# A gated linear attention and feed-forward kernel: weights loaded among the first tile and half of the second, the state update delayed by one to three steps, e and ln written two tiles ahead

## The chip, the cores and the metric

One core of one Trainium2 chip. The metric is the device time of one execution in microseconds (us). The profile's span is shorter than that time, by about 1.8 us in both kernels; the profiled run of each is compared with the other's. All times told here are of the fast state: one execution each of st_one_instruction and weights_behind_two_tiles was slow (over 1.5% above the same kernel's fastest) and is left out. Engines: PE is TensorE, DVE VectorE, ACT ScalarE, POOL GpSimd; SP issues the DMAs.

## The reference, cut to what matters

```python
f = 1.0 / (1.0 + np.exp(-f_logit))                 # B, H, S, D = 4, 8, 768, 48
for t in range(S):
    state = f[:, :, t, :, None] * state + np.einsum('bhd,bhe->bhde', k[:, :, t], v[:, :, t])
    y[:, :, t] = np.einsum('bhd,bhde->bhe', q[:, :, t], state)
x = y as (B*S, H*D)                                # 3072 x 384
out = np.maximum(x @ w1, x @ w2) @ w_out           # w1, w2: 384 x 1024; w_out: 1024 x 384
```

The kernel cuts the sequence into 6 chunks of 128 for each of 4 batches: 24 tiles, tile i being chunk i // 4 of batch i % 4. So tile i needs the state that tile i - 4 left.

## The kernel before: the parts concerned

The order of instructions is written by hand as words, `op n`. A prologue runs once; then STEP runs for i = 1, 2, ... with `op n` meaning that op on tile i + n. Whatever has been done is skipped. Each engine works through its own instructions in this order (ACT's x, e and ln of one step of before start at 69.97, 70.34 and 70.90), and SP issues the loads in this order.

```python
STEP = """
lk 5  lf 7  e 1  lq 5  ln 1  cum 1  d0 -1  ed 1  fl 1  ei 1  g0 -1  a 0  am 0  v 1  d1 -1
g1 -1  kpv 1  lv 5  o0 -1  y 0  x 0  qp 1  sa 0  o1 -1  xT 0  tmp 0  st 0  tr 1  xTe 0  tre 1
ob -1  out -1
"""
```

What the words do, by engine (cut to one line each; `...` marks cuts):

```python
# SP    lf lk lq lv: one tile's loads, 192 KB each in rows of 192 B;  lw1 lw2 lwo: weights;  out: store
# ACT   e:  nc.scalar.activation(e, f, AF.Exp, scale=-1.0)
#       ln: nc.scalar.activation(ell[:, :, 0:D], e, AF.Ln, bias=1.0)
#       ei, ed, fl: AF.Exp of cum;   g0, g1: Relu of d;   x: copy of y;   w2ca, woc: casts of weights
# PE    cum: matmul(lhsT=ut, rhs=ell) + four 1-column matmuls;   tr: 8 transposes of kp, qp
#       a: q k^T by head;   y: old state and am against q, v;   sa: k^T v (nothing for chunk 5)
#       xT: 3 transposes of x;   d0, d1: 12 matmuls wd x xT each;   o0, o1: 6 + 5 matmuls
#       w2T, w2o: from the weights, once;   warm: matmuls on zeros, nobody reads them
# DVE   v: cast of v;   kpv: k * ei;   am: a * mask;   tmp: sa + old state
#       xTe, tre, ob: copies out of PSUM;   w2Te, wd: once, from the weights
# POOL  qp: q * ed;   wdp 0: w1 - w2 for the first third

def m_st(i):                                     # POOL, two instructions
    ...
        for o in range(2):
            r, e = slice(o * DP, (o + 1) * DP), slice(o * D, (o + 1) * D)
            nc.gpsimd.tensor_mul(st_b[b][(c + 1) % 2][r, :, e], st[i]["tmp"][r, :, e],
                                 st[i]["fl"][r, :].unsqueeze(2).to_broadcast([DP, NP, D]))
```

max(h1, h2) is computed as relu(x (w1 - w2)) + x w2; `wd` is w1 - w2, and `w2o` is w2 w_out, made once. The PSUM pools: three rotating buffers for the attention (cum, tr, y, xT, sa), one for a, three for d, o and the weights.

## Time and profile before

| | before |
|---|---|
| time, median of 3 runs (lowest to highest) | 150.71 us (150.70 to 150.85) |
| span of the profiled run | 148.87 us |
| first feed-forward matmul (`d`) | 26.11 us |
| first `d` matmul of tile 2 | 36.29 us |
| tile 2 to tile 21 | 96.53 us in 19 steps, nearly all 5.09 |
| tile 21 to the end | 16.05 us |

Read it as three stretches. The prologue ends where the `d` matmuls of the tiles begin to come at equal distances. In the equal steps, a small saving counts 19 times. The end is one tile deep and has nothing behind it to fill its gaps.

### The profile page before, as it was taken

What the parts mean: (1) busy time and instruction counts of PE and PEld (TensorE: products, weight loads), DVE (VectorE), ACT (ScalarE), POOL (GpSimd) and SP (SyncE); (2) the same over time, 40 slices, a digit from 0 to 9 for tenths busy, and PEclk for the clock granted to TensorE, in tenths of its full rate; (3) what the DMA queues carried; (4) which work ended last, traced back from release to release, by engine and by line L of the source; (5) the groups of instructions that cost most, each with busy time, mean ns of one, the idle gap of its engine ahead of it and who ended that gap; (6) DMA issues with size and microseconds to landing.
All of it is one profiled execution on the core that took longest, in us unless ns stands there. A gap on an engine that the chain in (4) does not pass through costs nothing.

```text
span 148.9 us, 4490 instructions
## 1 busy us (share of the span) xinstructions
PE 134.7 (90%) x1835; PEld 101.6 (68%) x1835; DVE 107.4 (72%) x189; ACT 89.5 (60%) x201; POOL 50.7 (34%) x81
## 2 busy tenths in 40 slices
PE   0369879899999999999999999999999999999981
PEld 0134456677788778877887887788778877777760
DVE  7837985288787779778877887787778777756621
ACT  3435182967757676757766676757676756764430
POOL 8222263214334334432533352345225432201000
PEclk9999999999999999999999999999999999999999
DMA  5999999999998989999799999999999996101111
GB/s 100 197 224 390 395 341 220 200 195 174 221 198 168 228 174 218 200 223 224 155 230 194 236 216 208 222 198 230 206 209 183 228 230 177 54 3 53 57 53 53
DMA packets 105236, 28.60 MB, mean 192 GB/s; under 512 B 100352, under 2 KB 104448, under 8 KB 105216
## 3 DMA queue, kind: packets, MB, share of 16 engines
q1 hardware_dynamic: 105216, 28.32, 90.0%
q8 instruction: 14, 0.23, 0.7%
q14 instruction: 6, 0.05, 0.1%
HBM read 23.59 MB, written 4.72 MB: 190 GB/s over the span
## 4 chain that ended last, share of the span: by engine, by line
PE 72%; ACT 2%; DVE 1%; issue 0%
PE o L325 26%; PE d L307 22%; PE tr L222 6%; PE a L240 5%; PE cum L189 4%; PE y L285 3%; PE y L280 2%; PE xtp L295 2%; PE sa L254 2%; PE cum L191 1%; ACT ell L180 1%; ACT x L290 1%; ACT e L176 1%; DVE ob L330 0%; DVE qp L215 0%; DVE xT L299 0%
## 5 line engine op out<-in xcount | busy, mean ns | idle before, releaser
L307 PE MATMUL d<-xT,wd 128*128 128x128 bf16 x576 | 40.0, 219 | 0.7 <-DVE xT L299 0.4
L325 PE MATMUL o<-wo,gT 128*128 128x384 bf16 x192 | 38.9, 326 | 0.4 <-ACT gT L314 0.4
L269 POOL TENSOR_TENSOR st<-tmp,fl 64x192 bf16<-64x192 f32 x40 | 20.4, 509 | 45.0 <-DVE tmp L262 43.5
L314 ACT ACTIVATE gT<-d 128x512 bf16<-128x512 f32 x48 | 29.0, 607 | 10.2 <-PE d L307 10.1
L307 PEld LDWEIGHTS <-wd 128*128 128x128 bf16 x576 | 32.6, 97 | 3.4 <-issue 0.6
L245 DVE TENSOR_TENSOR am<-a,mask 128x1024 bf16<-128x1024 f32 x24 | 29.4, 1224 | 6.4 <-PE a L240 6.3
L215 POOL TENSOR_TENSOR qp<-qt,ed 128x384 bf16<-128x384 f32 x20 | 20.0, 998 | 21.1 <-POOL st L269 10.9
L325 PEld LDWEIGHTS <-gT 128*128 128x128 bf16 x192 | 17.3, 98 | 10.1 <-ACT gT L314 0.8
L290 ACT CAST x<-y 128x384 bf16<-128x384 f32 x24 | 11.5, 479 | 19.2 <-PE y L285 19.2
L231 DVE COPY trs<-tr 128x1024 bf16<-128x1024 bf16 (+1 forms) x25 | 16.6, 669 | 4.5 <-PE tr L222 2.7
L201 ACT ACTIVATE ed<-cum 128x384 f32<-128x384 f32 x24 | 11.7, 489 | 11.2 <-POOL st L269 9.1
L299 DVE COPY xT<-xtp 128x384 bf16<-128x384 bf16 x24 | 8.5, 356 | 11.5 <-PE xtp L295 11.5
L262 DVE TENSOR_TENSOR tmp<-sa,st 128x384 f32<-128x384 f32 x20 | 11.1, 556 | 6.4 <-issue 6.4
L325 PE MATMUL o<-w2o,xT 128*128 128x384 bf16 x72 | 15.6, 326 | 0.0
L197 ACT ACTIVATE ei<-cum 128x384 f32<-128x384 f32 x24 | 11.9, 497 | 6.2 <-PE cum L191 6.1
L330 DVE COPY ob<-o 128x384 f32<-128x384 f32 x24 | 13.2, 548 | 3.2 <-PE o L325 3.2
L176 ACT ACTIVATE e<-ft 128x384 f32<-128x384 f32 x24 | 12.7, 529 | 3.1 <-DMA ft<-in_f_logit_dram 3.1
L189 PE MATMUL cum<-ell,ut 128*128 128x384 bf16 x24 | 8.1, 338 | 6.5 <-ACT ell L180 6.3
L180 ACT ACTIVATE ell<-e 128x384 bf16<-128x384 f32 x24 | 12.6, 524 | 0.8
L191 PEld LDWEIGHTS <-ell 128*128 128x128 bf16 x96 | 6.0, 97 | 8.3 <-issue 5.6
L285 PE MATMUL y<-vb,am 128*128 128x48 bf16 x192 | 11.2, 183 | 0.2 <-DVE am L245 0.2
L285 PEld LDWEIGHTS <-am 128*128 128x128 bf16 x192 | 9.6, 96 | 2.3 <-DVE am L245 0.7
(50 smaller groups left out, 178.9 us busy)
## 6 DMA issues: line engine op xcount, KB each, us to landing
vt<-in_v_dram SPq DMA_DIRECT2D x24, 192.0 KB, 4.4
ft<-in_f_logit_dram SPq DMA_DIRECT2D x24, 192.0 KB, 4.3
qt<-in_q_dram SPq DMA_DIRECT2D x24, 192.0 KB, 4.7
kt<-in_k_dram SPq DMA_DIRECT2D x24, 192.0 KB, 4.4
out_dram<-ob SPq DMA_DIRECT2D x24, 192.0 KB, 3.3
w_f<-in_moe_w_dram SPq DMA_DIRECT2D x6, 512.0 KB, 8.3
wo_f<-in_moe_w_out_dram SPq DMA_DIRECT2D x2, 768.0 KB, 8.2
```

What stands on the lines that cost most here:

```text
L176: nc.scalar.activation(e, ld[i]["f"].rearrange("p h d -> p (h d)"), AF.Exp, scale=-1.0)
L180: nc.scalar.activation(ell[:, :, 0:D], st[i]["e"].rearrange("p (h d) -> p h d", h=H), AF.Ln, bias=1.0)
L189: nc.tensor.matmul(out=ps[:, 0:dm], lhsT=ut, rhs=ell[:, :, 0:D], start=True, stop=True)
L215: eng.tensor_mul(s["qp"][:, :, 0:D], ld[i]["q"], s["ed"].rearrange("p (h d) -> p h d", h=H))
L231: nc.vector.tensor_copy(s["tr"][:, n:n + len(sel)], psum.pop(("tr" + sel, i)))
L245: nc.vector.tensor_mul(am.rearrange("p o n c -> p (o n) c"), psum.pop(("a", i)).rearrange("p o n c -> p (o n) c"), mask)
L269: nc.gpsimd.tensor_mul(st_b[b][(c + 1) % 2][r, :, e], st[i]["tmp"][r, :, e], st[i]["fl"][r, :].unsqueeze(2).to_broadcast([DP, NP, D]))
L285: nc.tensor.matmul(out=y[:, ds], lhsT=am[:, o, p, :], rhs=vb[:, ds], start=(c == 0), stop=(c == 0 or o == 1))
L307: nc.tensor.matmul(out=ps[:, n, :], lhsT=wd[:, j, f * C:(f + 1) * C], rhs=st[i]["xT"][:, j, :], start=(j == 0), stop=(j == JG - 1))
L314: nc.scalar.activation(s["g"][:, half * 4:half * 4 + 4, :], psum.pop(("d", half, i)), AF.Relu)
L325: nc.tensor.matmul(out=psum["o", i], lhsT=l() if callable(l) else l, rhs=r, start=(n == 0), stop=(n == len(mms) - 1))
L330: nc.vector.tensor_copy(t, psum.pop(("o", i)))
```

## The change

The intent: load the weights earlier, so that the feed-forward part can begin after one tile rather than two; and give the chain e, ln, cum and the chain sa, tmp, st more time. Nothing is computed otherwise; 6 warm-up matmuls are left of 19.

```diff
 PROLOGUE = """
-lv 0  lf 0  lf 1  lq 0  lk 0  lk 1  lq 1  lv 1  lw2 0  lw2 1  lwo 0  lw2 2  lwo 1  lw1 0
-lq 2  lw1 1  lw1 2  lf 2  lv 3  lk 2  lv 2  lf 3  lk 3  lf 5  lq 3  lf 4  lk 4  lq 4  setup 0
... (11 more lines of the old prologue)
+setup 0  setup 2  setup 1  lf 1  lf 0  lq 0  lw2 2  lk 0  lw2 0  lw2 1  lv 0  lwo 1  e 0
+lwo 0  e 1  ln 1  lk 1  ln 0  cum 0  warm 5  lw1 0  w2ca 2  ei 0  lw1 2  ed 0  fl 0  qp 0
+cum 1  lw1 1  w2c 0  warm 1  ei 1  kp 0  ed 1  fl 1  lq 1  w2ca 1  lf 2  w2T 0  w2T 7  w2T 4
+tr 0  w2Te 7  w2Te 0  tre 0  w2T 5  w2T 1  a 0  lv 1  woc 2  am 0  w2Te 1  w2Te 4  v 0  lq 2
+woc 0  w2T 2  w2Te 5  y 0  w2Te 2  w2T 3  w2T 6  woc 3  lk 2  kpv 1  woc 1  w2Te 6  trk 1
+w2Te 3  trke 1  x 0  w2o 1  lf 3  wdp 0  xT 0  w2o 2  lv 2  wd 2  sa 0  xTe 0  w2o 0  w2oe 2
+lk 3  wd 1  w2oe 1  lq 3  qpv 1  d1 0  w2oe 0  tmp 0  trq 1  lf 4  e 2  d0 0  trqe 1  ln 2
+a 1  g0 0  lf 5  v 1  cum 2  g1 0  o0 0  ed 2  lv 3  qp 2  lq 4  lk 4  lk 5  lv 4  lq 5
+lv 5  lf 6  lk 6  lq 6  lf 7  lk 7  lv 6  lv 7  lq 7  lf 8  lv 8  lq 9  lq 8  lk 8  lf 9
 """
 STEP = """
-lk 5  lf 7  e 1  lq 5  ln 1  cum 1  d0 -1  ed 1  fl 1  ei 1  g0 -1  a 0  am 0  v 1  d1 -1
-g1 -1  kpv 1  lv 5  o0 -1  y 0  x 0  qp 1  sa 0  o1 -1  xT 0  tmp 0  st 0  tr 1  xTe 0  tre 1
-ob -1  out -1
+st -4  lv 2  d0 -1  out -4  cum 1  a 0  ed 1  d1 -1  lk 3  g0 -1  am 0  qp 1  ei 1  g1 -1
+o0 -1  lq 3  tmp -2  fl 1  y 0  lf 4  kpv 1  o1 -1  x 0  e 2  xT 0  tr 1  ln 2  xTe 0  sa -1
+tre 1  ob -1  v 1
 """
```

Four moves in STEP are not in the change's title and turn out to matter: cum goes behind d0, g0 goes before ei, and the cast v goes from the middle of the step to its end; the loads and the store get other places too.

And one move that is in the title is none. Written out by tile, ACT does x 8, e 10, ln 10, ed 10 in both kernels: `e 1` at the head of step 9 and `e 2` at the end of step 8 are the same e, behind the same x. What is new between ln and its cum is `d0`. Of the state update, sa comes one step later, tmp two, and st, in POOL's order, three.

More of the change, by code (lines that the diff above doesn't have):

```diff
@@ L17 @@
 PROLOGUE = """
-lv 0  lf 0  lf 1  lq 0  lk 0  lk 1  lq 1  lv 1  lw2 0  lw2 1  lwo 0  lw2 2  lwo 1  lw1 0
-lq 2  lw1 1  lw1 2  lf 2  lv 3  lk 2  lv 2  lf 3  lk 3  lf 5  lq 3  lf 4  lk 4  lq 4  setup 0
-lv 4  lk 5  lq 5  e 0  ln 0  lv 5  setup 2  setup 1  v 0  cum 0  ei 0  ed 0  fl 0  warm 3
-kp 0  qpv 0  tr 0  tre 0  e 1  ln 1  v 1  warm 3  a 0  am 0  cum 1  ei 1  ed 1  fl 1  kp 1
-warm 3  qpv 1  sa 0  warm 2  tmp 0  st 0  w2ca 0  y 0  x 0  tr 1  tre 1  xT 0  xTe 0  a 1
-am 1  w2c 1  sa 1  tmp 1  warm 1  st 1  warm 3  w2c 2  y 1  x 1  warm 2  w2T 0  w2Te 0  w2T 1
-w2Te 1  w2T 5  w2Te 5  w2T 2  w2Te 2  w2T 7  w2Te 7  w2T 3  w2Te 3  w2T 6  w2Te 6  woc 1
-woc 2  wdp 0  xT 1  xTe 1  woc 3  w2T 4  w2Te 4  woc 0  warm 1  wd 1  w2o 1  w2oe 1  w2o 0
-w2oe 0  warm 1  wd 2  w2o 2  w2oe 2  e 2  ln 2  d0 1  g0 1  d1 0  cum 2  ei 2  ed 2  fl 2
-d0 0  g0 0  kp 2  qpv 2  g1 0  o0 0  trk 2  trq 2  trke 2  trqe 2  o1 0  ob 0  v 2  a 2
-am 2  out 0  e 3  ln 3  cum 3  ei 3  ed 3  fl 3  v 3  lf 6  d1 1  g1 1  lk 6  lv 6  o0 1
-kp 3  qpv 3  lk 7  sa 2  tmp 2  st 2  y 2  x 2  tr 3  tre 3  lv 7  xT 2  xTe 2  lq 6  o1 1
-ob 1  lf 7  lq 7
+setup 0  setup 2  setup 1  lf 1  lf 0  lq 0  lw2 2  lk 0  lw2 0  lw2 1  lv 0  lwo 1  e 0
[7 more added lines that the diff above has]
+lv 5  lf 6  lk 6  lq 6  lf 7  lk 7  lv 6  lv 7  lq 7  lf 8  lv 8  lq 9  lq 8  lk 8  lf 9
 """
 STEP = """
-lk 5  lf 7  e 1  lq 5  ln 1  cum 1  d0 -1  ed 1  fl 1  ei 1  g0 -1  a 0  am 0  v 1  d1 -1
-g1 -1  kpv 1  lv 5  o0 -1  y 0  x 0  qp 1  sa 0  o1 -1  xT 0  tmp 0  st 0  tr 1  xTe 0  tre 1
-ob -1  out -1
+st -4  lv 2  d0 -1  out -4  cum 1  a 0  ed 1  d1 -1  lk 3  g0 -1  am 0  qp 1  ei 1  g1 -1
+o0 -1  lq 3  tmp -2  fl 1  y 0  lf 4  kpv 1  o1 -1  x 0  e 2  xT 0  tr 1  ln 2  xTe 0  sa -1
+tre 1  ob -1  v 1
 """
```

## The prediction

> **What bounds the kernel now.** I read the page first, then the chain of waits, the timeline of one steady step, the timeline of the first 40 us, and the landings of the DMA issues against the instruction that first uses each. The page:
>
> ```profile
> PE 134.7 (90%) x1835; PEld 101.6 (68%) x1835; DVE 107.4 (72%) x189; ACT 89.5 (60%) x201; POOL 50.7 (34%) x81
> ...
> PE   0369879899999999999999999999999999999981
> ...
> DMA  5999999999998989999799999999999996101111
> ```
>
> TensorE (PE) is full from slice 9 on, and the DMA engines are busy almost as long. There are two regimes: a prologue (weights, first tiles) and about twenty equal steps. The first `d` matmul of each tile marks the steps: tile 2 at 36.29 us, then 41.21, 46.30, 51.39 and so on every 5.09 to 5.10 us to tile 21 at 132.82: 19 steps in 96.53 us. From there to the end of the span are 16.05 us; the time of 150.7 is 1.8 us over the span.
>
> A full PE row does not show that PE sets the step, since ends of matmuls are modelled. The chain of waits between 120 and 134 us passes through ScalarE (ACT) once a step:
>
> ```profile
> 125.96 0.48 ACT x L290
> 126.44 0.43 ACT e L176
> ...
> 126.89 0.53 ACT ell L180
> ...
> 127.47 0.32 PE cum L189
> ```
>
> `x` waits for the y matmuls, `e` and `ln` (it writes `ell`) stand behind `x` on ACT, and `cum` waits for `ln`. The same in mid-kernel, from the timeline (columns: start, duration, engine):
>
> ```profile
> 69.97 0.48 ACT L290 CAST x<-y 128x384 bf16<-128x384 f32 x1 [0.75 <-PE y L285]
> 70.34 0.53 ACT L176 ACTIVATE e<-ft 128x384 f32<-128x384 f32 x1
> 70.90 0.52 ACT L180 ACTIVATE ell<-e 128x384 bf16<-128x384 f32 x1
> ...
> 71.48 0.32 PE L189 MATMUL cum<-ell,ut 128*128 128x384 bf16 x1
> ```
>
> `ell` ends at 71.42 and `cum` starts 0.06 later. In the step before, the last transpose starts at 66.222 and `cum` at 66.390; a transpose follows another in 0.056, so PE lost 0.112. It is a loop: cum to y 3.01, y to x 0.57, x to end of `ell` 1.45, to `cum` 0.06: 5.09. A check that this loop and not PE work sets the step: tiles 20 and later have no `sa` matmuls (0.17 of PE), yet the step stays 5.09.
>
> The prologue is bound by DMA, then by making the weights:
>
> ```profile
> 21.19 2.35 POOL L152 TENSOR_TENSOR wd<-w_f 128x1024 bf16<-128x1024 f32 x1 [0.84 <-DMA w_f<-in_moe_w_dram]
> ...
> 23.29 1.34 DVE L152 TENSOR_TENSOR wd<-w_f 128x1024 bf16<-128x1024 f32 x1 [1.06 <-DMA w_f<-in_moe_w_dram]
> ...
> 25.31 1.22 DVE L152 TENSOR_TENSOR wd<-w_f 128x1024 bf16<-128x1024 f32 x1 [0.68 <-DMA w_f<-in_moe_w_dram]
> ```
>
> The last weight lands at 25.28, behind both first tiles and q of tile 2; its subtraction releases the first feed-forward matmuls at 26.6. Then the loads of tiles 2 to 5 come in just in time: f3 lands 0.20 us before its use, q4 0.22, q6 0.16. Later leads grow to several us.
>
> [...]a DVE product of two SBUF tensors takes 0.55 alone, 1.08 beside POOL:
>
> ```profile
> 13.45 1.00 POOL L210 TENSOR_TENSOR kp<-kt,ei 128x384 bf16<-128x384 f32 x1 [4.03 <-ACT ei L197]
> ...
> 13.78 1.08 DVE L215 TENSOR_TENSOR qp<-qt,ed 128x384 bf16<-128x384 f32 x1 [0.19 <-ACT ed L201]
> ```
>
> It ended 0.41 after POOL did. (The first line is from POOL's timeline, the second from DVE's.) [...]transposes come every 0.107 us at 9.5 to 10.2 and every 0.056 from 14.5 on[...]. The granted clock row does not show this state. [...]192 KB of tile load in rows of 192 B takes 1.0 us (196 GB/s), while a slice full of weights moves 390 GB/s.
>
> **The change, part by part.**
>
> *e and ln two tiles ahead.* The work is the same, but `ln` now ends a step before its `cum`, and `cum` moves behind `d0`. This breaks the loop above. The PE sum of a step from starts in the trace: d0 0.67, cum 0.26, a 0.42 (0.19 of it switching to and from 48-row tiles), d1 0.68, first half of o 0.975, y 0.375, rest of o 0.81, x transposes 0.17, k/q transposes 0.45, sa 0.17: 4.98. So at most 0.11 a step, 2.1 us over 19.
>
> *State update delayed.* `sa` moves behind the transposes, `tmp` comes a step later still and `st` opens the step four later, just before its reader. `sa` between the transposes and the next `d0` is useful filler: xT transpose to next d0 is 0.17+0.45+0.17 = 0.79, and near the end of before, where nothing filled the hole, the same path took 0.78 (136.75 to 137.53). In exchange x has less cover, only the 0.81 of o1; near the end the old kernel runs y, o1, xT in this order and xT starts with no gap (140.68 + 5 x 0.1625 = 141.49). On POOL, `st` no longer waits for its `tmp` and follows qp at once. From d0 = 0: cum 0.67, ed starts 1.17 and ends 1.66, qp 1.73 to 2.72, st to 3.80. On DVE: am 1.47 to 2.69, tmp to 3.17, kp from about 3.1. So st lies over kp, which has two SBUF inputs; by the 0.41 above kp ends near 4.21 and its transposes are due at 4.31. I book 0.02 to 0.03 of lost gain, a step of 5.00 and 19 x 0.09 = 1.7 us gained.
>
> *Prologue.* All eight weight loads now stand among the loads of tile 0 and k1; q1 and v1 come after them. DMA: first landing 3.7; five more tile loads before the last weight at 1.05 each, 5.3; the weights took 13.26 (11.05 to 25.28 less 0.97 for q2). Last weight: 22.2, 3.1 earlier than now. Then at 1.0 each: q1 23.2, f2 24.2, v1 25.2, q2 26.2, k2 27.2, f3 28.2, v2 29.2, k3 30.2, q3 31.2, f4 32.2, f5 33.2, v3 34.2, q4 35.2, v5 40.2 (40.32 now, the same bytes). Engines: w2_1 lands about 11.5; the ACT cast (1.06) ends at 12.6. Then 24 transposes with DVE evictions of 0.35, mixed with am, trs, v and kp of tile 0/1, end near 19. wo lands by 16.7 and its last three casts on ACT (0.83 each) end near 19 too. Then w2o, 3 x 1.31 of PE with small work between, to 23.4. Meanwhile w1_0 lands at 19.2, POOL subtracts until 21.55, and [...]the DVE subtraction of w1_2 ends near 22.65, xT to 22.95, the last subtraction 24.2. d1 of tile 0 starts there, rather than 26.1 with d of tile 1.
>
> But less is done by then: tile 1 still owes q transposes, a, am, y, x, xT. One tile alone fills PE badly: trq 25.2, d0 25.9, a 26.4, o0 to 27.4, am 1 to 27.7, y and o1 to 28.8, ed/ei of tile 2 behind g on ACT to 28.1, kp 2 behind POOL's qp to 29.1, transposes 29.6. d0 of tile 1: 29.4. The next step, with no old state in y, is 4.8: d0 of tile 2 at 34.0 to 34.4, take 34.2, against 36.29. Loads: q3 (31.2) may be as late as 32.7, v3 (34.2) as late as 35, q4 as late as 37. They hold, though a prologue over 1 us faster would hit them. Gain 2.1 us.
>
> Sum: 36.29 - 2.1 + 96.53 - 1.7 + 16.05 = 145.1 span, plus 1.8: **146.9**. After the prologue list, four loads and a store took 4.83 a step (stores of tile 4 to 14 in before), below 5.00, so the transfers stay ahead; stores held back four steps cost nothing.
>
> **Rivals.** (a) *Cold PE.* Warm-up matmuls fall from 19 to 6 and PE is idle in parts of 10.6 to 19.[...] (b) [...]If st delays kp by more than I worked out, the loop cum, ed, qp, st, kp, transposes lasts and the step stays near 5.09: 148.6. For: only 0.1 of slack[...]. (c) *DMA is the bound.* If the early loads take 1.1 rather than 1.0 (f6 to f9 in before did), tiles 3 and 4 slip by 1 us: 148. (d) *All gain as worked out, and a fuller prologue*: 33.0 (v3's limit) and steps of 4.98: 145.2.
>
> **Range and chances.** Rivals a to c each cost 1 to 1.7 and seldom all fall together; d bounds the good side. 145.2 to 148.7 should hold it 8 times in 10. 2% faster is 147.7; 0.72 for it, 0.27 for within 2%, 0.01 for slower: the work is the same, and no loop has grown beyond 5.09 by my sums.
>
> **What would show it right or wrong.** Right: no ACT in the chain of mid-kernel; d0 every 4.98 to 5.02; last weight landing near 22.2; first d near 24.2; d0 of tile 2 near 34.2; kp on DVE lengthened from 0.55 to about 1.1, and no gap before the k transposes. Wrong: w2o matmuls spaced 0.32 instead of 0.163 (rival a); a gap before the transposes with kp as releaser and a step over 5.05 (b); e, qp or v waiting for DMA after 30 us (c). If d0 of tile 2 comes after 35.5, the prologue is mis-sized.

## The result, and the profile after

| | before | after | predicted |
|---|---|---|---|
| time, median of 4 runs each | 150.78 us | 146.91 us (146.31 to 147.11) | 146.9 |
| span of the profiled run | 148.87 | 145.10 | 145.1 |
| last weight lands | 25.28 | 21.42 | 22.2 |
| first `d` matmul | 26.11 | 24.73 | 24.2 |
| first `d` matmul of tile 2 | 36.29 | 34.76 | 34.2 |
| tile 2 to tile 21 | 96.53 | 94.06 | 94.8 |
| tile 21 to the end | 16.05 | 16.28 | 16.05 |

The ratio is 0.9735 with a 95% interval of 0.9705 to 0.9765. Ratios here are the mean time of one kernel's fast runs over that of the other's of the same rounds, so not quite the ratio of the medians.

The page of after, the lines that answer to the first ones of before:

```profile
PE 131.0 (90%) x1822; PEld 102.6 (71%) x1822; DVE 105.8 (73%) x188; ACT 88.3 (61%) x202; POOL 54.2 (37%) x81
...
PE   0186599999999999999999999999999999999980
...
DMA  4999998999898999979899997999999998991111
```

PE is full from slice 6 rather than 9; DMA is busy to the end of the loads as before. The share of PE in the span is the same 90% in both, though the span is 3.8 us shorter: shares don't show what happened.

The chain of waits of after in mid-kernel (start, duration, what):

```profile
73.65 0.17 PE xtp L291 x3
73.81 0.45 PE tr L218 x8
74.26 0.17 PE sa L250 x4
74.43 0.67 PE d L303 x12
75.10 0.16 PE cum L185
```

ACT is gone from it. `sa` stands between the transposes and `d`, `cum` behind `d0`, and each starts as the one before ends: the step is the sum of PE's work, 4.96 us (4.79 in the first chunk, where y has no old state). ACT in the same place, from the timeline of after, and the `cum` that reads this `ell`:

```profile
72.87 0.48 ACT L286 CAST x<-y 128x384 bf16<-128x384 f32 x1 [0.53 <-PE y L281]
73.24 0.53 ACT L172 ACTIVATE e<-ft 128x384 f32<-128x384 f32 x1
73.80 0.52 ACT L176 ACTIVATE ell<-e 128x384 bf16<-128x384 f32 x1
```

```profile
74.94 0.33 PE L185 MATMUL cum<-ell,ut 128*128 128x384 bf16 x1
```

`ell` ends at 74.32 and is read at 74.94, 0.61 us later; in before it was 0.06 us. (The chain counts a piece from the end of the one before, so it has this cum at 75.10.) The loop through ACT is still there, but it now has 0.61 us to spare, since the 0.67 us of `d0` come before cum.

The prologue of after, PE, then DVE and POOL (timeline):

```profile
19.18 2.77 PE L163 MATMUL w2op<-wo,w2T 128*128 128x384 bf16 x8
21.75 0.37 PE L291 MATMUL xtp<-ident,x 128*128 128x128 bf16 x3
21.96 1.46 PE L163 MATMUL w2op<-wo,w2T 128*128 128x384 bf16 x8
...
23.43 1.46 PE L163 MATMUL w2op<-wo,w2T 128*128 128x384 bf16 x8
```

```profile
20.12 2.12 DVE L148 TENSOR_TENSOR wd<-w_f 128x1024 bf16<-128x1024 f32 x1 [0.23 <-DMA w_f<-in_moe_w_dram]
...
22.44 1.21 DVE L148 TENSOR_TENSOR wd<-w_f 128x1024 bf16<-128x1024 f32 x1
```

```profile
18.82 2.35 POOL L148 TENSOR_TENSOR wd<-w_f 128x1024 bf16<-128x1024 f32 x1 [6.85 <-DMA w_f<-in_moe_w_dram]
```

The first eight of the 24 w2o matmuls take 2.77 us, the next eight 1.46: one matmul every 0.320 us, then every 0.163. PE's pace doubled only near 21.8; 3.6 us of work without a gap, from 6.84 to 10.42, had left it at the slower one (eight transposes in 0.83 us from 12.39 on). The row of granted clock shows none of it, it says 9 in every slice. The last subtraction for `wd` ended at 23.65; `d` started at 24.73, when w2o was done. So w2o, not `wd`, set the start. The first DVE subtraction took 2.12 rather than 1.21: it lay over POOL's, which ended at 21.17, and ended 1.07 after it.

### The profile page after: what moved, and what is told of

It is laid out like the page before. It is cut to its first block, busy times and chain, and to the rows that moved or that the text cites. A ratio compares the mean times of both kernels' runs of the same rounds, so it can differ in the third digit from the quotient of the medians.

```text
span 145.1 us, 4444 instructions
## 1 busy us (share of the span) xinstructions
PE 131.0 (90%) x1822; PEld 102.6 (71%) x1822; DVE 105.8 (73%) x188; ACT 88.3 (61%) x202; POOL 54.2 (37%) x81
## 4 chain that ended last, share of the span: by engine, by line
PE 87%; DMA 5%; SPq 3%; DVE 2%; ACT 1%; issue 0%
PE o L321 30%; PE d L303 24%; PE tr L218 8%; PE a L236 6%; DMA w_f<-in_moe_w_dram 5%; PE w2op L163 4%; PE y L281 3%; PE xtp L291 3%; PE cum L185 3%; PE y L276 2%; PE sa L250 2%; SPq L122 2%; PE w2tp L155 1%; PE cum L187 1%; SPq L130 1%; DVE am L241 1%
## 5 line engine op out<-in xcount | busy, mean ns | idle before, releaser
L211 POOL TENSOR_TENSOR qp<-qt,ed 128x384 bf16<-128x384 f32 x23 | 23.0, 1001 | 69.7 <-ACT ed L197 62.1
L303 PEld LDWEIGHTS <-wd 128*128 128x128 bf16 x576 | 33.2, 98 | 3.2 <-issue 0.6
L265 POOL TENSOR_TENSOR st<-tmp,fl 64x192 bf16<-64x192 f32 x40 | 24.3, 608 | 1.5
L295 DVE COPY xT<-xtp 128x384 bf16<-128x384 bf16 x24 | 8.6, 357 | 21.8 <-PE xtp L291 21.8
L206 DVE TENSOR_TENSOR kp<-kt,ei 128x384 bf16<-128x384 f32 x23 | 13.5, 585 | 0.3 <-ACT ei L193 0.3
```

The costliest lines, as they stand in the source:

```text
L206: eng.tensor_mul(s["kp"][:, :, 0:D], ld[i]["k"], s["ei"].rearrange("p (h d) -> p h d", h=H))
L211: eng.tensor_mul(s["qp"][:, :, 0:D], ld[i]["q"], s["ed"].rearrange("p (h d) -> p h d", h=H))
L303: nc.tensor.matmul(out=ps[:, n, :], lhsT=wd[:, j, f * C:(f + 1) * C], rhs=st[i]["xT"][:, j, :], start=(j == 0), stop=(j == JG - 1))
```

## The experiments

Theory: the 5.09 of the step was a loop y, x, e, ln, cum, which the change opens, and the prologue gains what the earlier weights allow. Rivals: the delayed state update gives the steps' gain (the profile of before puts 9.1 us of ed's and 10.9 us of qp's idle time down to POOL's st); the loads' order alone gives it; PE's slower pace at the start or the loads of tiles 3 and 4 limit the prologue. Each kernel was timed beside before on the same chip; "d2" is the first `d` matmul of tile 2.

| run | time us | ratio to before (95%) | d2 | steady step |
|---|---|---|---|---|
| old_prologue_new_step | 148.58 | 0.9838 (0.9811 to 0.9865) | 36.55 | 4.96 |
| new_prologue_old_step | 150.63 | 0.9979 (0.9966 to 0.9992) | 36.61 | 5.09 |
| only_e_ln_ahead | 151.73 | 1.0045 (1.0014 to 1.0076) | 36.36 | 4.98, two of 6.98 and 6.41 |
| only_state_delayed | 150.96 | 1.0009 (0.9989 to 1.0028) | 36.52 | 5.09 |
| only_cum_behind_d0 | 155.01 | 1.0271 (1.0244 to 1.0298) | 36.95 | 5.28 |
| cum_behind_d0_and_state | 151.25 | 1.0037 (1.0019 to 1.0055) | 36.79 | 5.06 |
| e_ln_ahead_f_early | 149.12 | 0.9877 (0.9829 to 0.9926) | 36.62 | 4.98, one of 5.50 |
| new_prologue_old_step_v_late | 157.42 | 1.0418 (1.0376 to 1.0461) | 35.59 | 5.58 |
| st_one_instruction (wrong result on purpose) | 147.13 | 0.9711 (0.9644 to 0.9779) | 35.00 | 4.96 |
| warm_filled | 146.51 | 0.9715 (0.9687 to 0.9743) | 34.28 | 4.96 |
| weights_behind_two_tiles | 154.91 | 1.0283 (1.0239 to 1.0327) | 42.30 | 4.96 |
| weights_last_order_kept | 153.24 | 1.0122 (1.0069 to 1.0176) | 41.13 | 4.96 |

### The two halves apart: old_prologue_new_step and new_prologue_old_step

```diff
 old_prologue_new_step = kernel before with
-STEP of before
+STEP of after
 new_prologue_old_step = kernel after with
-STEP of after, FIRST_STEP = 1
+STEP of before, FIRST_STEP = 0      (so that st of tile 0 is done)
```

> Prologue of before, steps of after. My theory (the step was a loop through ScalarE, 5.09 us; now it is the sum of TensorE's work, 4.96): d0 of tile 2 at about 36.0, then steps of 4.96, span about 146.4, time about 148.2, ratio to before 0.983. Rival (the new steps need the new prologue's order of loads, and DMA is what is really gained): steps above 5.0 in the first ten tiles, time 149.5 or more.

> Prologue of after, steps of before (the step loop begins one earlier, so that the state update of tile 0 is done). My theory: d0 of tile 2 near 35.0, steps of 5.09, time about 149.4, ratio 0.991. With the run of the new steps alone the two parts should add up to the whole, 3.9 us. Rival (parts interact): the sum of the two gains differs from 3.9 by more than 0.7 us.

The new steps alone gave 2.3 us, as the theory had it: 4.96 from tile 3 on. The new prologue alone gave 0.2 instead of 1.3; 2.3 and 0.2 are not 3.9, so the rival "the parts interact" was right there. (Its profiled run was the slowest of 20, 151.5; its d2 may be some tenths late.) DVE's timeline in that run shows where it went:

```profile
29.73 0.40 DVE L180 CAST vb<-vt 128x384 bf16<-128x384 f32 x1 [1.85 <-DMA vt<-in_v_dram]
...
34.98 0.36 DVE L180 CAST vb<-vt 128x384 bf16<-128x384 f32 x1 [1.17 <-DMA vt<-in_v_dram]
```

In the old step the cast of v stands before kp. v2, v3 and v4 were each cast 0.02 us after landing, and kp and the transposes stood behind. In after, v is cast at the end of the step and the same loads have 1.3 to 1.9 us to spare.

### Which part of the step: only_e_ln_ahead, only_state_delayed

```diff
 only_e_ln_ahead (on before)
-lk 5  lf 7  e 1  lq 5  ln 1  cum 1  ...
+lk 5  lf 7  e 2  lq 5  ln 2  cum 1  ...
 only_state_delayed (on before)
-lk 5 ... kpv 1 ... qp 1  sa 0  o1 -1  xT 0  tmp 0  st 0  tr 1  xTe 0 ...
+st -4  lk 5 ... tmp -2  kpv 1 ... qp 1  o1 -1  xT 0  tr 1  sa -1  xTe 0 ...
```

> Kernel before with one edit in the step: e and ln are issued for the tile two ahead; cum stays before d0, the state update stays where it was. My theory: this alone opens the loop, steps of 4.97 to 4.98, no gap before cum, time about 148.5, ratio 0.985. Rival (the delayed state update gives the gain): steps stay 5.09, time 150.7.

> Kernel before with sa one, tmp two and st four steps later, e and ln as before. My theory: the loop y, x, e, ln, cum is untouched, so steps stay 5.09 and the time is 150.7 within 0.3, although sa no longer stands between y and o. Rival (the profile's own reading, ed and qp waiting for GpSimd's st, 9.1 and 10.9 us in total): the step falls below 5.05, time 149.7 or less.

The delayed update alone changes nothing: steps of 5.09, as expected. So the 20 us that the profile puts down to st as releaser were no cost of st. The last steps of before, where no st is left, agree: `ed` begins 0.50 us after the start of `cum` there (132.56 to 133.06), as in mid-kernel (66.39 to 66.89). The releaser that the profile names was only the last event near it.

e and ln ahead alone bring the step to 4.98, as expected, and still the kernel is 0.9 us slower, which I had not expected. ACT in that run:

```profile
42.98 0.52 ACT L176 ACTIVATE e<-ft 128x384 f32<-128x384 f32 x1 [3.00 <-DMA ft<-in_f_logit_dram]
...
49.40 0.52 ACT L176 ACTIVATE e<-ft 128x384 f32<-128x384 f32 x1 [2.43 <-DMA ft<-in_f_logit_dram]
```

e is wanted one step earlier, and f6 and f7 weren't there: 3.0 and 2.4 us of waiting, more than the 19 savings of 0.11. In this run e and ln do come a step earlier: `ell` ends 4.92 us before its cum. Neither before nor after has that. So the run shows that the loop sets the step, not by which move the change opens it.

### The loads that belong to it: e_ln_ahead_f_early

```diff
 on only_e_ln_ahead: f6 and f7 go before k5 and behind v5 in the queue, q6 before k6;
 lf 8 at the prologue's end, and in STEP
-lk 5  lf 7  ...
+lf 8  lk 5  ...
```

> Kernel before with e and ln two tiles ahead, and the f loads of tiles 6, 7 and 8 and on moved ahead in the queue. My theory (the run without the moved loads lost 3.0 and 2.4 us to waits for f6 and f7): steps of 4.98 from tile 3 on with no step over 5.6, time 148.3 to 149.0, ratio 0.986. Rival (the loads of those steps are short whichever comes first): two or three steps over 5.6 and time 149.8 or more.

Measured 149.12, just above the range, with one step of 5.50 (f8 landed 0.02 us before its use) and the others 4.98; from tile 20 on, without sa, they fall to 4.81, where those of before stayed at 5.09. So the theory held: with its loads moved, the earlier e is worth 1.2%. With them where they were, it costs 0.5%.

### cum behind d0: only_cum_behind_d0, cum_behind_d0_and_state

```diff
 only_cum_behind_d0 (on before)
-... cum 1  d0 -1  ed 1 ...
+... d0 -1  cum 1  ed 1 ...
 cum_behind_d0_and_state: the same, and the edit of only_state_delayed
```

> Kernel before with one edit: cum moves behind d0 in the step; e and ln stay one tile ahead. My theory: ln then has 0.67 us to spare and the loop through ScalarE is open, but nothing but 0.61 us of transposes lies between xT and d0, whose eviction takes 0.78, so TensorE loses 0.17 there: steps of 5.13 to 5.15, time about 151.6, ratio 1.006. Rival (opening the loop is all that counts): steps of 4.97, time 148.6.

> As the run before, and the state update delayed, so that sa fills the hole between the transposes and d0; e and ln still one tile ahead, loads as before. My theory: steps of 4.96 to 4.98 without any earlier e, and no wait for f loads, so 148.5, ratio 0.985. Rival (e and ln two ahead is needed): steps stay at 5.05 or more.

Both steps were longer than I expected, 5.28 and 5.06. PE in the first:

```profile
75.95 0.65 PE L325 MATMUL o<-w2o,xT 128*128 128x384 bf16 x3
76.59 0.66 PE L325 MATMUL o<-wo,gT 128*128 128x384 bf16 x3
...
78.83 0.39 PE L222 MATMUL tr<-ident,qp 128*128 128x128 bf16 x4
79.22 0.83 PE L307 MATMUL d<-xT,wd 128*128 128x128 bf16 x12
```

Three matmuls of `o` take 3 x 0.1625, so the next was due at 76.44 and came at 76.59: 0.15 lost to g0, which stands behind ed, fl and ei on ACT, and these now start later since cum does. Four transposes take 4 x 0.056, so `d` was due at 79.05 and came at 79.22: 0.17, the hole that I had expected, where xT is being copied. 4.96 + 0.15 + 0.17 = 5.28. With sa in the hole only g0's wait is left: 5.06. So three moves go together: cum behind d0, sa into the hole behind the transposes, g0 before ei. After has all three, and old_prologue_new_step reaches 4.96 with them. That g0 is worth the last 0.10 is read from the trace; no run has that move alone. Both runs also lost 0.3 to 0.4 us once, from tile 4 to tile 5 (steps of 5.58 and 5.42), where `ed` began late; that wasn't followed up. The second run's rival (e and ln two ahead is needed) got its number, but not for its reason: e has the same place in this run as in after, and `ell` ends 0.61 us before its cum in both.

### VectorE and GpSimd lengthen each other's work: new_prologue_old_step_v_late, st_one_instruction

```diff
 new_prologue_old_step_v_late (on new_prologue_old_step)
-... a 0  am 0  v 1  d1 -1 ... ob -1  out -1
+... a 0  am 0  d1 -1 ... ob -1  v 1  out -1
 st_one_instruction (on after)
-for o in range(2):
-    nc.gpsimd.tensor_mul(st_b[...][r, :, e], tmp[r, :, e], fl[r, :]...to_broadcast([DP, NP, D]))
+nc.gpsimd.tensor_mul(st_b[...], tmp, fl...to_broadcast([C, NP, 2 * D]))
```

> Prologue of after, steps of before with one word moved: the cast of v of the next tile goes from before kp to the end of the step. My theory (in the run without this, DVE stood in order behind v2, v3 and v4, each cast 0.02 us after its landing, and kp and the transposes behind it): those waits go, d0 of tile 2 at 35.0 to 35.6 rather than 36.61, tile 3 not over 5.2 later, steps of 5.09 after that, time 149.0 to 149.5, ratio 0.990. Rival (other waits of the old step hold the new prologue's gain back): d0 of tile 2 stays over 36.2, time 150.2 or more.

> Kernel after with the state update as one GpSimd instruction over 128 partitions and 384 elements instead of two over 64 and 192; wrong result on purpose, since the blocks off the diagonal are kept. My theory ([...]kp slipped in between the two): kp on VectorE now takes 0.95 to 1.1 us instead of 0.56, ending about 0.41 after the update; it still ends before its transposes are due, so steps stay within 0.03 of 4.96 and the time at 146.9. Rival[...]: kp stays 0.56.

The first did to the early tiles what I expected: d2 at 35.59, steps of 4.92 there. Then, unexpected, every step took 5.58. DVE and POOL (two answers):

```profile
74.87 1.18 DVE L180 CAST vb<-vt 128x384 bf16<-128x384 f32 x1
75.97 1.21 DVE L241 TENSOR_TENSOR am<-a,mask 128x1024 bf16<-128x1024 f32 x1
```

```profile
74.83 1.00 POOL L211 TENSOR_TENSOR qp<-qt,ed 128x384 bf16<-128x384 f32 x1 [0.69 <-POOL st L265]
```

The cast takes 0.35 alone, and has one SBUF input, where the prediction spoke of products of two. Here it starts 0.04 after qp and takes 1.18; qp ends at 75.83, the cast 0.22 later. am, and y behind it, slip with it. In after the same cast is over before qp begins, because cum and with it ed and qp come 0.67 later in the step:

```profile
75.37 0.35 DVE L180 CAST vb<-vt 128x384 bf16<-128x384 f32 x1
...
77.32 0.56 DVE L206 TENSOR_TENSOR kp<-kt,ei 128x384 bf16<-128x384 f32 x1
```

```profile
76.00 1.00 POOL L211 TENSOR_TENSOR qp<-qt,ed 128x384 bf16<-128x384 f32 x1 [2.72 <-ACT ed L197]
76.96 1.29 POOL L265 TENSOR_TENSOR st<-tmp,fl 64x192 bf16<-64x192 f32 x2
```

Here kp lies over st, as I predicted, yet it is not longer. st is two instructions: in this step 76.956 to 77.461 and 77.536 to 78.242. kp ended 0.416 after the first of them, as the product beside POOL in the prologue of before did (0.41), and before the second, which took 0.71 rather than 0.50. With st as one instruction:

```profile
77.56 0.88 DVE L206 TENSOR_TENSOR kp<-kt,ei 128x384 bf16<-128x384 f32 x1
```

```profile
77.21 0.83 POOL L263 TENSOR_TENSOR st<-tmp,fl 128x384 bf16<-128x384 f32 x1
```

kp takes 0.88 and ends 0.41 after st. I expected 0.95 to 1.1; the one st takes 0.83, less than the two of 0.50. The step stays 4.96, since kp is still done when its transposes are due. What I had left out is that st is two instructions: kp ends 0.416 after the first of the two, and 0.41 after the one.

### The prologue: warm_filled, weights_behind_two_tiles, weights_last_order_kept

```diff
 warm_filled (on after)
-cum 1  lw1 1  w2c 0  warm 1  ei 1 ...
+cum 1  lw1 1  w2c 0  warm 5  ei 1 ...
 weights_behind_two_tiles (on after, loads only)
-f1 f0 q0 w2:2 k0 w2:0 w2:1 v0 wo:1 wo:0 k1 w1:0 w1:2 w1:1 q1 f2 v1 ...
+v0 f0 f1 q0 k0 k1 q1 v1 w2:0 w2:1 wo:0 w2:2 wo:1 w1:0 q2 w1:1 w1:2 f2 k2 ...
 weights_last_order_kept (on after, loads only)
+v0 f0 f1 q0 k0 k1 q1 v1 w2:2 w2:0 w2:1 wo:1 wo:0 w1:0 w1:2 w1:1 f2 q2 k2 ...
```

> Kernel after with four more warm-up matmuls in the idle time before the weight transposes (5 rather than 1). My theory (the first w2o group ran at 0.320 us a matmul[...] on the path): all w2o matmuls at 0.163, first d at 23.6 to 23.9 rather than 24.7, time 146.0 to 146.3, ratio to before 0.969. Rival (the loads of tiles 3 and 4 take the place at once: k4 had 0.19 us of lead): first d earlier, but d0 of tile 3 at 39.3 or later and time 146.7 to 146.9.

> Kernel after with the loads of the first tiles and the weights put back into the order of before, nothing else. My theory: last weight lands near 25.3 rather than 21.4, the first d some 3 us later, tile 1 then ready at once, so part of it is given back; d0 of tile 2 at 36.5 to 37.5, steps unchanged at 4.96, time 148.7 to 149.5. Rival (the order of the compute words makes the prologue's gain): under 147.4.

> Kernel after, its weights loaded behind tiles 0 and 1 as in before, but in after's own order among themselves, so that ScalarE's first cast isn't held up by the fourth weight as in the run with before's order. My theory: each weight lands 2.5 to 3.6 us later, the first d at 27.2 to 27.8 rather than 24.7, d0 of tile 2 at 37 to 37.8, steps 4.96, time 149.2 to 149.9, ratio 0.992. Rival (the place of the weights matters little, the stream of loads is as long either way): under 147.8.

**warm_filled** had PE at the faster pace from 13.05 on (eight transposes in 0.45 us, 0.83 in after): the w2o matmuls come every 0.163, but for one wait (the first eight take 1.63, the others 1.46). PE (timeline):

```profile
19.04 1.63 PE L163 MATMUL w2op<-wo,w2T 128*128 128x384 bf16 x8
...
24.30 0.79 PE L303 MATMUL d<-xT,wd 128*128 128x128 bf16 x11 [0.64 <-DVE wd L148]
```

w2o was done at 23.44, 1.29 earlier than in after, but `d` then waited for the last subtraction until 24.30; in this run the weights landed 0.6 later than in after (the last at 22.04). f3 and f2 had 0.02 and 0.08 us to spare. d2 came 0.48 earlier and the span was 0.46 shorter. The time, 146.51 against 146.91, points the same way, but the intervals of the two ratios overlap: not clear of noise. So both had a share: the slower pace was on the path, and right behind it stand the loads. What is read here is one execution of each: the four of after had mean granted clocks of 0.999, 0.973, 0.974 and 0.999 and took 146.31 to 147.11; whether PE's pace in the prologue was the same in each was not shown.

**The two orders of loads** cost far more than the 2 to 3 us I expected from the later landings, at 154.91 and 153.24. The words of the prologue are made for one order of landing. In the first, the cast that ACT has in front, of w2:2, waited 9.6 us for a weight that now came as the fourth, and ei, ed and all of tile 0 stood behind it. In the second w2:2 came first, but still 5.4 us later than in after, behind two tiles:

```profile
13.11 1.05 ACT L139 CAST w_h<-w_f 128x1024 bf16<-128x1024 f32 x1 [5.65 <-DMA w_f<-in_moe_w_dram]
```

and the first `d` came at 31.09. A part of this is DVE beside POOL again:

```profile
22.16 2.05 DVE L180 CAST vb<-vt 128x384 bf16<-128x384 f32 x1
```

```profile
21.65 2.35 POOL L148 TENSOR_TENSOR wd<-w_f 128x1024 bf16<-128x1024 f32 x1 [4.38 <-DMA w_f<-in_moe_w_dram]
```

A cast of 0.35 took 2.05 beside the subtraction, with y, w2T and w2o behind it. So the gain of the place of the weights can't be read from these two runs as a number on its own; they show that it can't be had or undone apart from the order of the engines' work.

No version clearly beats after; warm_filled may be some 0.4 us faster.

## Why the prediction was right, and where it was not

The time, 146.91, was predicted as 146.9, which is closer than the working deserves. Of the sum 36.29 - 2.1 + 96.53 - 1.7 + 16.05, three terms were off and cancel: the prologue gained 1.53, not 2.1; the steps 2.47, not 1.7; the end lost 0.23 (0 predicted). (Rival d's numbers sum to 145.3 rather than 145.2, which changes nothing.)

- **The loop through ACT bounds the steps**: right. The e_ln_ahead runs, which open it by another way than after, reached 4.98, only_state_delayed stayed at 5.09, and the chain of after has no ACT in it.
- **"`ln` now ends a step before its `cum`"**: wrong. It ends 0.61 us before it, and x, e, ln, ed follow each other on ACT as in before. The other half of that sentence, cum behind `d0`, opens the loop by itself (in only_cum_behind_d0 `ell` ends 0.77 us before its cum). The sum asked only that the loop open, so it was luck that it came out right.
- **The PE sum of 4.98**: right to 0.02. 4.98 is what the e_ln_ahead runs have, with cum before `d0` as in the sum. In after, cum stands between `d0` and a, and d0, cum and a take 1.34 us up to d1, rather than 1.36.
- **0.02 to 0.03 a step given back because POOL's st delays kp** (rival b in small): wrong. I took st for one block of 1.08 us. kp ends before the second of its two instructions and keeps 0.56; no gap follows. The step came out 0.04 below the 5.00 predicted, 0.76 us in 19; half of this is the loss that did not come, half the PE sum.
- **sa fills the hole behind the transposes**: right, shown by 5.28 with the hole and 5.06 without (0.17 of the difference is the hole, the rest g0's shorter wait).
- **The last weight at 22.2, the last subtraction at 24.2**: 21.42 and 23.65, both early; the first DVE subtraction (2.12 us) ended 1.07 after POOL's, where the prediction has 1.10.
- **w2o, "3 x 1.31 of PE", done at 23.4**: the failed term of the prologue. The first third ran at half the pace, 8 x (0.320 - 0.163) = 1.26 us more; w2o ended at 24.73 and set the start of `d`, 0.53 later than the 24.2 predicted, and d2 is later by the same 0.56. I had a cold PE as rival (a) and left it out of the sum. It happened: warm_filled shows that without it the next limit, the subtraction, lies only some 0.5 to 1 us before.
- **The loads hold**: right but close. q3 had 0.22 and k4 0.19 us, and v5 landed at 41.97, not 40.2; rival (c) did not happen, though the new prologue with the old step ran into it at once.
- **The end unchanged**: off by 0.23, since cum (0.26) now lies behind `d0`: for the last tile it moved from one side of my cut to the other. That much the prologue's gain is flattered.
- **PE's two paces in before**, 0.107 and 0.056 us a transpose, and a clock row that doesn't show them: right. The change lies behind 12.26: the cum there still takes 0.29 us to the next matmul, as the one at 6.25 did (0.28), against 0.16 in mid-kernel; the warm-up matmuls come every 0.215 from 12.70 on.
- **What I did not see**: the cast of v at the step's end and g0 before ei are no ornament. Without the first the new prologue loses its gain (0.2 us left of the 1.3 that I expected); with the first alone in the old step, the cast beside qp costs 0.49 a step.

## What to carry to other kernels

When a step's period is longer than its fullest engine's work (5.09 against 4.98 of PE here), look for a loop through another engine by adding up start-to-start distances in one step; a check is a stretch where work falls away and the period stays. Moving an instruction earlier or later in an engine's order moves its loads' deadline, what runs beside it on another engine and its successors' start with it (3.00 us of waiting for f6 here, a cast of 1.18 rather than 0.35), so such a change works as a set: single parts of this one were slower than nothing. Before an effect is put down to a move, write out each engine's order by tile: a word that moved across the step's edge and counts one tile more has not moved. Where one engine's instruction takes longer beside another's, count instructions, not blocks of work (kp took 0.56 over the two of st, 0.88 over one).
